# Banded attention and a gated layer on one core: a batch's sinks in one load, own slots for the last outputs, the last slice in halves

## The chip, the cores and the metric

The kernel runs on one core of a Trainium2 chip. The metric is the device time of one execution in microseconds (us). Before the change it is 776.53 us, the median of three runs (776.24 to 777.06). A difference below 0.2% (about 1.5 us) cannot be told from no change.

## The reference

Attention over 4 batches, 8 heads, 768 positions, head size 64. A query sees the first `n_sink` = 4 keys (the sinks) and a causal window of 128 keys. The head outputs, laid side by side, are the 3072 x 512 input x of a gated layer with 1536 hidden columns:

```
scores = where(is_sink | in_window, q @ k.T / 8, -1e9)
x      = (softmax(scores) @ v), heads side by side          # 3072 x 512
out    = (sigmoid(x @ w_gate) * (x @ w_val)) @ w_out        # 3072 x 512
```

The weights arrive as float64 and are decoded on the chip.

## The kernel before

Work is cut into attention units (`attend`: batch, head, 256 queries; 96 of them) and into the gated layer (`feed`) over eight chunks of tokens: four of 256, then four of 512. A feed runs over 12 slices of 128 hidden columns (`f` from 0 to `NF - 1`). Precise products are made of two parts: a tile is split into a rounded part (`hi`, `gh`) and its remainder (`lo`, `gl`), and TensorE multiplies three of the four combinations. The remainders of the weights are spilled to DRAM (`wlo_d`) and read back slice by slice into eight `lo` slots.

In the last four chunks (`feed_pair`) one slice goes as follows: 72 matmuls into the accumulators `m`; VectorE adds them up into `cv` and `th` (two halves of 256 tokens), ScalarE takes tanh of `th`; VectorE multiplies `th` and `cv`; `gated` rounds the product (`gh`) and subtracts (`gl`); `downs` multiplies `gh` and `gl` with the output weights into four accumulators (two called `o`, two called `a`, one per 128 tokens). TensorE normally works on the next slice's `m` while a slice passes through the vector engines. After the last slice, `out_tiles` copies each accumulator by ScalarE into a tile `w` (tag `w2`, two slots) and SP stores it. A small check (`bad`, `count`, `flag`, `total`) follows, with a branch that all engines take.

For each batch `sinks` loads the 16 first rows of v for all heads, repeated eight times over the 128 partitions, into `raw` (also a `w2` slot; the trace calls it `w`), from which ScalarE or VectorE and GpSimd make `vshl`.

The order of all instructions is made before the launch: `Plan.run` (lines 353 to 546) simulates the engines with a table of costs and due times and records, for each engine, the operation of lowest priority number that is ready. An operation with several `ways` goes to whichever engine is free. `GAP` sits in a rule there: an operation is held back when one that is more urgent by more than `GAP` will be due within 0.6 of its duration. An attention unit's priority is its number, so `GAP` = 2.0 compares units at least three apart. Up to 130 us the plan also puts matmuls of `ident` on TensorE where it expects the engine to be idle (`m<-ident`, fillers without use). All operations are recorded by a helper at line 618, so every row of the trace has that line.

Of the kernel before, what the change touches and what calls it, by code (L numbers as in the profile page):

```python
# [9 lines left out]
F32 = mybir.dt.float32  # L10
F32R = mybir.dt.float32r
# [4 lines left out]
ALU = mybir.AluOpType  # L16
# [4 lines left out]
NS = 16  # L21
# [3 lines left out]
CHUNKS = ((0,), (1,), (2,), (3,), (4, 5), (6, 7), (8, 9), (10, 11))  # L25
# [10 lines left out]
FLIP = 1  # L36
HOLD = 0.6
HELD = 800000.0
GAP = 2.0
LATER = 45000.0  # L40
HALVED = 30000.0
TSTEP = 8000.0
# [50 lines left out]
BUFS = {}  # L93
# [456 lines left out]
def kernel(  # L550
# [2 lines left out]
    qk: bass.AP,  # L553
    v: bass.AP,
    vt: bass.AP,
    marks: bass.AP,
    w_gate: bass.AP,
    w_val: bass.AP,
# [8 lines left out]
    B, H, S, D = v.shape  # L567
    DM, DF, _ = w_gate.shape
    DO = w_out.shape[1]
    NC = DM // 128  # L570
    NF = DF // 128
# [15 lines left out]
    class Late:  # L587
# [5 lines left out]
        def tile(self, *args, **kw):  # L593
            if self.pool is None:
                first.close()
                self.pool = main.enter_context(tc.tile_pool(name="p3", bufs=1))
            return self.pool.tile(*args, **kw)
# [10 lines left out]
    plan = Plan()  # L608

    class InOrder:  # L610
# [9 lines left out]
    PE, V, A, G, Q = (  # L620
        InOrder(e) for e in (nc.tensor, nc.vector, nc.scalar, nc.gpsimd, nc.sync)
    )
# [10 lines left out]
    def act(cols, psum=False):  # L633
        return 120 + 0.9 * cols
# [7 lines left out]
    def dma(prio, ns, fn, r=(), w=(), start=0.0, behind=None):  # L642
        return plan.op(prio, [("Q", ISSUE, fn)], r, w, dma=ns, start=start, behind=behind)
# [43 lines left out]
    def tile(shape, dtype, tag, bufs, pool=None):  # L687
# [7 lines left out]
    VSHL = {}  # L695
# [15 lines left out]
            out=nums()[:, 0:4],  # L711
            in_=marks.bitcast(I32).rearrange("(o x) -> o x", o=1).broadcast_to([128, 4]),
# [125 lines left out]
    def sinks(b, u):  # L838
        if not b:
            for y in range(2):  # L840
                for x in V0:
                    zero(u + 0.5 + y, x[y], 3 * D, lambda x=x, y=y: x[y]()[:, :, (1 - y) * D : (2 - y) * D], 4)
            for x in SK0:
                zero(u + 0.4, x, 128, x)
            for x in VS0:
                zero(u + 0.3, x, H * D, x)
            for t, x in enumerate(VS0):
                for y in range(2):
                    o = 64 * y + NS * t
                    dma(  # L850
                        u + 0.5, 91.0, lambda x=x, y=y, o=o: Q.dma_start(
                            out=x()[o : o + NS, :, y * D : y * D + D],
                            in_=v[b, y::2, 0:NS, :].rearrange("h p d -> p h d"),
                        ), w=[(x, o)],
                    )
        raw = tile([128, H, D], F32, "w2", BUFS["w2"])
        for i in range(0 if b else 1, 2):
            VSHL[b, i] = tile([128, H // 2, 2 * D], F32R, "vshl", 2, const)
        u = max(u, PLAIN) + SINKP
        for o in range(0, 128, NS):  # L860
            dma(
                u, 91.0, lambda o=o: Q.dma_start(
                    out=raw()[o : o + NS], in_=v[b, :, 0:NS, :].rearrange("h p d -> p h d"),
                ), [READY2], [(raw, o)] + [VSHL[b, i] for i in range(2) if b and (b, i) in VSHL],
            )
        for i in range(0 if b else 1, 2):
            hs = slice(i * H // 2, i * H // 2 + H // 2)
            both = VSHL[b, i]
            x, hi = lambda hs=hs: raw()[:, hs], lambda both=both: both()[:, :, 0:D]
            copy(u, H // 2 * D, hi, x, [raw], [both, READY2])  # L870
            rest(
                u, H // 2 * D, lambda both=both: both()[:, :, D : 2 * D], x, hi, [raw, both], [both]
            )
# [482 lines left out]
    def out_tiles(ci, g, T, O):  # L1356

        for j, acc in enumerate(O):
            ot = tile([128, DO], F32, "w2", BUFS["w2"])
            r = (g + j) * 128  # L1360
            plan.op(
                -1000.0 + ci + 1,
                [("A", act(DO, True), lambda acc=acc, ot=ot: A.mul(out=ot(), in_=acc(), mul=0.5))],
                [acc], [ot],
            )
            dma(ci, 728.0, lambda ot=ot, r=r: Q.dma_start(out=out[r : r + 128], in_=ot()), [ot])

    def feed(ci):
# [103 lines left out]
    def downs(pe, f, O, gh, gl, woh, wol, when):  # L1472
        for j, acc in enumerate(O):

            def down(j=j):
                ts = slice(j * 128, j * 128 + 128)
                for i, (x, w) in enumerate(((gh, woh()[:, 0]), (gh, wol()), (gl, woh()[:, 0]))):
                    PE.matmul(
                        O[j](), lhsT=x()[:, ts], rhs=w,
                        start=f == 0 and i == 0, stop=f == NF - 1 and i == 2,  # L1480
                    )

            plan.op(
                pe + when[j] / NF, [("PE", 3 * mac(DO), down)], [gh, gl, woh, wol], [acc]
            )
# [50 lines left out]
    def feed_pair(ci, tcs, f, O):  # L1536
        pr = -1000.0 + ci + f / NF
        pe = 10000.0 + ci + f / NF
        n, k = tcs
        gh_, vh_, woh, th_ = wres[f]  # L1540
        t12h, t12l, glo, tlo, vlo, wol = fetch(pr, f, 0, 1, 3, 2, 4, 5)
        ma, mb = (Tile(MS, None, F32, "m", BUFS["m"]) for _ in range(2))
        th = tile([128, 2, 256], F32, "th", BUFS["th"])
        cv = tile([128, 2, 256], F32, "cv", BUFS["cv"])
        X = lambda *key: lambda i: (XH[key]()[:, i], XL[key]()[:, i])
        xs = lambda *key: [XH[key], XL[key]]
        gw, vw, tw = (lambda i, x=x: x()[:, i] for x in (gh_, vh_, th_))
        reg = lambda m, i: lambda: m()[:, i * 256 : i * 256 + 256]
        u2, c1, t0, t1 = (lambda i=i, x=x: x()[:, i] for x in (cv, th) for i in range(2))

        def add(out, m, i, x, r, w):
            plan.op(
                pr, [("V", vec(256), lambda: V.tensor_tensor(
                    out=out(), in0=reg(m, i)(), in1=x(), op=ALU.add
                ))],
                [m] + r, w,
            )

        def turn(i, src, r):
            plan.op(  # L1560
                pr, [("A", act(256, True), lambda: A.activation(
                    out=th()[:, i], in_=src(), func=AF.Tanh, scale=0.5
                ))],
                r, [(th, i)],
            )

        product(pe, ma, 0, 256, gw, 0, four(glo), 0, X(n, 0), True, False, [gh_, glo] + xs(n, 0), [ma, GROUPS])
        product(
            pe + 0.05 / NF, ma, 1, 256, four(t12h), 2, four(t12l), 2, X(k, "s2"), False, True,
            [t12h, t12l] + xs(k, "s2"), [ma],  # L1570
        )
        plan.op(
            pr, [("A", act(256, True), lambda: A.copy(out=u2(), in_=reg(ma, 0)()))],
            [ma], [cv, th],
        )
        add(u2, ma, 1, u2, [], [(cv, 0)])
        product(
            pe + 0.2 / NF, mb, 0, 256, tw, 0, four(tlo), 0, X(k, "s3"), True, False, [th_, tlo] + xs(k, "s3"),
            [mb, GROUPS],
        )  # L1580
        product(
            pe + 0.25 / NF, mb, 1, 256, four(t12h), 0, four(t12l), 0, X(k, "s1"), False, False,
            [t12h, t12l] + xs(k, "s1"), [mb],
        )
        add(t1, mb, 0, u2, [(cv, 0)], [(th, 1)])
        add(c1, mb, 1, t1, [(th, 1)], [(cv, 1)])
        product(
            pe + 0.4 / NF, ma, 0, 256, gw, 2, four(glo), 2, X(n, 1), False, True, [gh_, glo] + xs(n, 1), [ma],
        )
        product(  # L1590
            pe + 0.45 / NF, ma, 1, 256, tw, 2, four(tlo), 2, X(k, 1), True, True,
            [th_, tlo] + xs(k, 1), [ma],
        )
        turn(0, reg(ma, 0), [ma])
        add(t1, ma, 1, t1, [], [(th, 1)])
        turn(1, t1, [])
        product(
            pe + 0.6 / NF, mb, 1, 256, vw, 2, four(vlo), 2, X(k, "s4"), False, True,
            [vh_, vlo] + xs(k, "s4"), [mb],
        )  # L1600
        add(u2, mb, 1, u2, [], [(cv, 0)])
        plan.op(
            pr, [("V", two(512), lambda: V.scalar_tensor_tensor(
                out=th(), in0=th(), scalar=1.0, in1=cv(), op0=ALU.add, op1=ALU.mult
            ))],
            [cv], [th],
        )
        gh, gl = gated(pr, 512, th)
        downs(pe, f, O, gh, gl, woh, wol, (1.3, 1.5, 1.65, 1.7))

    decoding = iter(range(3 * NF))

# [6 lines left out]
    u = 0  # L1619
# [42 lines left out]
        general(tc, qk, v, ident, nsk, win, wres, wlo_d, out)  # L1662


_INS = ["qk", "v", "vt", "marks", "moe_w_gate", "moe_w_val", "moe_w_out"]
_OUTS = [((3072, 512), "float32")]


# [40 lines left out]
```

## Time and profile before

| what | value |
|---|---|
| median of three runs | 776.53 us |
| the profiled execution | 771.55 us |
| its span, first to last instruction | 769.8 us |
| TensorE busy, VectorE, ScalarE, GpSimd | 97%, 79%, 62%, 66% |
| granted TensorE clock, mean of the span | 0.997 |
| end of SP's last store issue (758.96 + 3.78), end of the span | 762.74, 769.8 us |

The profiled execution took 771.55 us, of which 1.75 us lie outside the span. It is 4.98 us below the median of the timed runs. The busy share of TensorE is read by stages: an engine that is busy nearly all the time can only be helped where it waits.

### The profile page before, as it was taken

Reading aid. Unit: us, or ns where it says so; the run is one execution under the profiler, and the core shown is the slowest. Engines: PE = TensorE matmul, PEld = TensorE weight load, DVE = VectorE, ACT = ScalarE, POOL = GpSimd, SP = SyncE. Lnnn points to the kernel's source line nnn. Section 1 sums busy time; section 2 is a strip of 40 time slices with the busy share of each in tenths; the row PEclk is TensorE's granted clock in tenths of the full one; section 3 lists DMA queues with packets and bytes.
Section 4 is the critical chain, followed back from the end, with each engine's and each line's share of the span. In section 5 each row is a group of like instructions: output and inputs, shape, how many; then the busy total and the mean of one; then the engine's idle time right before and its main releaser. Section 6 shows DMA issues by size and latency. Waiting matters only on the chain.

```text
span 769.8 us, 16294 instructions
## 1 busy us (share of the span) xinstructions
PE 747.2 (97%) x4986; PEld 675.6 (88%) x4986; DVE 606.8 (79%) x1776; ACT 473.4 (62%) x1339; POOL 507.1 (66%) x648
## 2 busy tenths in 40 slices
PE   7999999999999999999999999999999999999994
PEld 6867777999899999989999989999999999999993
DVE  5979988987899999969988999689999874433331
ACT  7889898756765777647666665467776642322221
POOL 3664677887999989847787977467976854412120
PEclk9999999999999999999999999999999999999998
DMA  6898987999999876677767776867687656776661
GB/s 165 230 293 262 335 270 237 374 310 303 337 327 311 271 236 203 207 249 234 242 217 222 248 250 198 255 210 237 208 290 243 179 170 209 226 227 205 199 198 59
DMA packets 120878, 185.57 MB, mean 241 GB/s; under 512 B 23248, under 2 KB 45264, under 8 KB 120784
## 3 DMA queue, kind: packets, MB, share of 16 engines
q1 hardware_dynamic: 120784, 184.45, 75.9%
q8 instruction: 42, 0.69, 0.4%
q14 instruction: 52, 0.43, 0.2%
HBM read 159.24 MB, written 25.17 MB: 240 GB/s over the span
## 4 chain that ended last, share of the span: by engine, by line
PE 67%; DVE 10%; DMA 4%; ACT 2%; POOL 2%; issue 1%; SPq 0%; ACTq 0%; POOLq 0%; DVEq 0%
PE m L618 37%; PE a L618 18%; PE o L618 12%; DMA out_dram<-w 1%; DVE ws L618 1%; DVE P L618 1%; DVE th L618 1%; POOL wt L618 1%; DMA wst<-in_moe_w_gate_dram 1%; DVE hi L618 1%; DVE gl L618 1%; DVE vhl L618 1%; DMA wst<-in_moe_w_out_dram 1%; DMA lo<-wlo_d 1%; DVE xf L618 1%
## 5 line engine op out<-in xcount | busy, mean ns | idle before, releaser
L618 PE MATMUL m<-ws,lo 128*128 128x256 f32 x1344 | 288.4, 283 | 1.7 <-DMA lo<-wlo_d 0.9
L618 PE MATMUL m<-ws,ws 128*128 128x256 f32 x1536 | 289.3, 284 | 0.2 <-ACT th L618 0.2
L618 PEld LDWEIGHTS m<-ws,ws 128*128 128x128 f32 x1536 | 245.1, 189 | 12.1 <-issue 0.5
L618 PEld LDWEIGHTS m<-ws,lo 128*128 128x128 f32 x1344 | 215.0, 189 | 2.7 <-DMA lo<-wlo_d 1.7
L618 POOL TENSOR_SCALAR_AFFINE_SELECT wt<-wt 128x512 fp32r<-128x512 f32 (+3 forms) x192 | 124.7, 651 | 42.9 <-DVE wt L618 18.7
L618 POOL TENSOR_TENSOR gl<-th,gh 128x512 fp32r<-128x512 f32 (+1 forms) x35 | 39.3, 1124 | 105.7 <-ACT gh L618 88.7
L618 ACT ACTIVATE P<-P,negm_all 128x144 f32<-128x144 f32 x192 | 78.9, 411 | 29.4 <-DVE negm_all L618 27.7
L618 ACT ACTIVATE th<-m 128x256 f32<-128x256 f32 x96 | 36.6, 381 | 74.7 <-DVE th L618 71.1
L618 DVE TENSOR_TENSOR cv<-m,cv 128x256 f32<-128x256 f32 x96 | 40.1, 418 | 51.0 <-ACT cv L618 33.0
L618 ACT CAST gh<-th 128x512 fp32r<-128x512 f32 (+1 forms) x81 | 42.7, 527 | 52.9 <-DVE th L618 51.1
L618 POOL TENSOR_TENSOR ws<-ws,ws 128x512 fp32r<-128x512 f32 (+1 forms) x53 | 66.9, 1270 | 8.3 <-DVE ws L618 5.5
L618 PE MATMUL o<-ws,gh 128*128 128x512 f32 x168 | 67.7, 403 | 1.3 <-ACT w L618 0.7
L618 PE MATMUL o<-ws,gl 128*128 128x512 f32 x168 | 66.2, 394 | 0.7 <-POOL gl L618 0.7
L618 PE MATMUL o<-lo,gh 128*128 128x512 f32 x168 | 65.8, 392 | 0.0
L618 DVE CUSTOM_DVE_ANT_0 P<-a,am 128x144 f32<-128x144 f32 x192 | 58.3, 306 | 9.2 <-PE a L618 2.6
L618 PE MATMUL a<-wt,vhl 128*128 128x256 f32 (+2 forms) x282 | 60.9, 326 | 0.2
L618 POOL TENSOR_TENSOR kl<-qkT,hi 128x400 fp32r<-128x400 f32 (+1 forms) x56 | 58.8, 1050 | 1.8
L618 ACT CAST hi<-qkT 128x656 fp32r<-128x656 f32 (+1 forms) x70 | 49.2, 703 | 10.5 <-PE a L618 8.6
L618 PEld LDWEIGHTS a<-wt,vhl 128*128 128x128 f32 x282 | 47.3, 189 | 8.5 <-POOL wt L618 2.2
L618 POOL TENSOR_TENSOR P<-P,rs 128x288 f32<-128x288 f32 x46 | 35.5, 774 | 28.5 <-DVE rs L618 24.6
L618 POOL TENSOR_TENSOR hi<-qkT,hi 64x256 fp32r<-64x256 f32 x53 | 41.6, 784 | 14.0 <-issue 3.2
L618 DVE COPY_PREDICATED a<-tri,a 128x128 f32<-128x128 int32 x160 | 45.4, 284 | 3.8 <-PE a L618 3.4
(142 smaller groups left out, 1737.8 us busy)
## 6 DMA issues: line engine op xcount, KB each, us to landing
lo<-wlo_d SPq DMA_DIRECT2D x396, 256.0 KB, 3.7
wlo_d<-ws SPq DMA_DIRECT2D x72, 256.0 KB, 4.3
qkT<-in_qk_dram SPq DMA_DIRECT2D x52, 328.0 KB, 4.2
qkT<-in_qk_dram SPq DMA_DIRECT2D x24, 264.0 KB, 3.8
wst<-in_moe_w_gate_dram SPq DMA_DIRECT2D x12, 512.0 KB, 4.6
wst<-in_moe_w_val_dram SPq DMA_DIRECT2D x12, 512.0 KB, 5.2
wst<-in_moe_w_out_dram SPq DMA_DIRECT2D x12, 512.0 KB, 5.2
out_dram<-w SPq DMA_DIRECT2D x24, 256.0 KB, 3.9
```

The source lines that it names most:

```text
L618: return lambda *a, **kw: tc.keep_in_program_order(op(*a, **kw))
```

## The change

Four edits.

1. The host passes one more array, `vs`: for each batch the 16 sink rows of all heads, 2 KB per row, repeated eight times to 128 rows. `sinks` loads it by one DMA of 128 rows instead of eight DMAs of 16 x 8 pieces of 256 bytes.
2. The outputs of the last chunk go to `xf` slots (five) instead of `w2` (two), and may be copied by VectorE as well as by ScalarE.
3. The last slice of the last chunk goes through multiply, round and subtract in two halves of 256 tokens (second half first), the subtraction on VectorE; the twelve output matmuls are ordered by half, the `gh` ones ahead of the `gl` ones.
4. `GAP` is 1.5 instead of 2.0, so that the rule also compares units two apart.

```
-GAP = 2.0
+GAP = 1.5
...
-        for o in range(0, 128, NS):
-            dma(
-                u, 91.0, lambda o=o: Q.dma_start(
-                    out=raw()[o : o + NS], in_=v[b, :, 0:NS, :].rearrange("h p d -> p h d"),
-                ), [READY2], [(raw, o)] + [VSHL[b, i] for i in range(2) if b and (b, i) in VSHL],
-            )
+        dma(
+            u, 728.0, lambda: Q.dma_start(out=raw(), in_=vs[b].rearrange("p (h d) -> p h d", h=H)),
+            [READY2], [raw] + [VSHL[b, i] for i in range(2) if b and (b, i) in VSHL],
+        )
...
-            ot = tile([128, DO], F32, "w2", BUFS["w2"])
+            last = ci == len(CHUNKS) - 1
+            ot = tile([128, DO], F32, *(("xf", BUFS["xf"]) if last else ("w2", BUFS["w2"])))
...
+            ways = [
+                ("A", act(DO, True), lambda acc=acc, ot=ot: A.mul(out=ot(), in_=acc(), mul=0.5)),
+                (
+                    "V", vec(DO), lambda acc=acc, ot=ot: V.tensor_scalar(
+                        out=ot(), in0=acc(), scalar1=0.5, scalar2=None, op0=ALU.mult
+                    ),
+                ),
+            ]
+            plan.op(-1000.0 + ci + 1, ways if last else ways[:1], [acc], [ot])
...
+        if ci == len(CHUNKS) - 1 and f == NF - 1:
+            last_slice(pr, pe, O, th, cv, woh, wol)
+            return
...
+    def last_slice(pr, pe, O, th, cv, woh, wol):
+
+        gh = tile([128, 512], F32R, "gh", BUFS["gh"])
+        gl = tile([128, 512], F32R, "gl", BUFS["gl"])
+        for h in (1, 0):
+            cs = slice(h * 256, h * 256 + 256)
+            t = lambda h=h: th()[:, h]
+            plan.op(
+                pr, [("V", two(256), lambda h=h, t=t: V.scalar_tensor_tensor(
+                    out=t(), in0=t(), scalar=1.0, in1=cv()[:, h], op0=ALU.add, op1=ALU.mult
+                ))],
+                [(cv, h)], [(th, h)],
+            )
+            hi, lo = lambda cs=cs: gh()[:, cs], lambda cs=cs: gl()[:, cs]
+            plan.op(
+                pr, [("A", act(256), lambda hi=hi, t=t: A.copy(out=hi(), in_=t()))],
+                [(th, h)], [(gh, h)],
+            )
+            plan.op(
+                pr, [("V", two(256), lambda hi=hi, lo=lo, t=t: V.tensor_tensor(
+                    out=lo(), in0=t(), in1=hi().bitcast(F32), op=ALU.subtract
+                ))],
+                [(th, h), (gh, h)], [(gl, h)],
+            )
+        n = 0
+        for h in (1, 0):
+            for x, ws in ((gh, (lambda: woh()[:, 0], lambda: wol())), (gl, (lambda: woh()[:, 0],))):
+                for j in (2 * h, 2 * h + 1):
+
+                    def down(j=j, x=x, ws=ws):
+                        for w in ws:
+                            PE.matmul(
+                                O[j](), lhsT=x()[:, j * 128 : j * 128 + 128], rhs=w(),
+                                start=False, stop=x is gl,
+                            )
+
+                    n += 1
+                    plan.op(
+                        pe + (1.7 + 0.01 * n) / NF, [("PE", len(ws) * mac(DO), down)],
+                        [(x, h), woh, wol], [O[j]],
+                    )
```

Edits 1 and 4 alter the plan's inputs near the start, and nearly the whole order of the instructions on every engine comes out differently. Work moves between engines that share an operation (of the full-width subtractions `gl`, 25 stand on VectorE before and 19 after), the stores and loads keep their number but for the sinks (32 loads become 4), and the fillers go from 26 to 31 (each is two rows of the trace).

TensorE at the end of the program, before; `o` and `a` are the four accumulators, `gh` and `gl` the rounded part and the remainder of the last slice, `ws` and `lo` the output weights:

```order
L618 MATMUL a_10523<-ws_1765,gl_11270 128x512
L618 MATMUL o_10474<-ws_2039,gh_11325 128x512
L618 MATMUL o_10474<-lo_11249,gh_11325 128x512
L618 MATMUL o_10474<-ws_2039,gl_11327 128x512
L618 MATMUL o_10500<-ws_2039,gh_11325 128x512
L618 MATMUL o_10500<-lo_11249,gh_11325 128x512
L618 MATMUL o_10500<-ws_2039,gl_11327 128x512
L618 MATMUL a_10515<-ws_2039,gh_11325 128x512
```

The same place after; `a_10486` and `a_10494` hold the second half of the tokens:

```order
L619 MATMUL a_10486<-ws_1967,gh_11293 128x512
L619 MATMUL a_10486<-lo_11220,gh_11293 128x512
L619 MATMUL a_10494<-ws_1967,gh_11293 128x512
L619 MATMUL a_10494<-lo_11220,gh_11293 128x512
L619 MATMUL o_10445<-ws_1967,gh_11293 128x512
L619 MATMUL o_10445<-lo_11220,gh_11293 128x512
L619 MATMUL a_10486<-ws_1967,gl_11302 128x512
L619 MATMUL a_10494<-ws_1967,gl_11302 128x512
L619 MATMUL o_10471<-ws_1967,gh_11293 128x512
L619 MATMUL o_10471<-lo_11220,gh_11293 128x512
L619 MATMUL o_10445<-ws_1967,gl_11302 128x512
L619 MATMUL o_10471<-ws_1967,gl_11302 128x512
```

A matmul of `gl` stood third before; now six matmuls of `gh` come ahead of the first one.

VectorE at the end, before; the multiply of the last slice is the third row:

```order
L618 TENSOR_TENSOR th_11290<-m_89,th_11290 128x256
L618 TENSOR_TENSOR cv_11278<-m_90,cv_11278 128x256
L618 SCALAR_TENSOR_TENSOR th_11290<-th_11290,cv_11278 128x512
L1656 CAST flag<-count 1x4
L1658 TENSOR_REDUCE total<-flag 1x1
```

The same place after:

```order
L619 TENSOR_TENSOR th_11261<-m_89,th_11261 128x256
L619 SCALAR_TENSOR_TENSOR th_11261<-th_11261,cv_11249 128x256
L619 TENSOR_TENSOR cv_11249<-m_90,cv_11249 128x256
L619 SCALAR_TENSOR_TENSOR th_11261<-th_11261,cv_11249 128x256
L619 TENSOR_TENSOR gl_11302<-th_11261,gh_11293 128x256 x2
L619 TENSOR_SCALAR xf_11311<-a_10486 128x512
L619 TENSOR_SCALAR xf_11320<-o_10445 128x512
L1705 CAST flag<-count 1x4
L1707 TENSOR_REDUCE total<-flag 1x1
```

The first half's multiply stands ahead of the last sum `cv`, both subtractions and two of the four output copies are VectorE's now, and the check's `flag` waits behind them. ScalarE keeps the two roundings and the other two copies.

SP's queue around the first batch's sinks, before (`w_210` is `raw`, `qkT` and `vhl` are loads of the attention):

```order
L618 DMA wst_204<-in_moe_w_out_dram 128x1024
L618 DMA w_210<-in_v_dram 16x8x64 x3
L618 DMA qkT_160<-in_qk_dram 64x528
L618 DMA w_210<-in_v_dram 16x8x64
L618 DMA vhl_111<-in_vt_dram 128x2x64
L618 DMA qkT_98<-in_qk_dram 64x528
L618 DMA w_210<-in_v_dram 16x8x64
L618 DMA vhl_153<-in_vt_dram 128x2x64
L618 DMA w_210<-in_v_dram 16x8x64 x3
L618 DMA qkT_116<-in_qk_dram 64x528
```

The same place after:

```order
L619 DMA wst_204<-in_moe_w_out_dram 128x1024
L619 DMA w_210<-in_vs_dram 128x512
L619 DMA qkT_164<-in_qk_dram 64x528
L619 DMA vhl_111<-in_vt_dram 128x2x64
L619 DMA qkT_98<-in_qk_dram 64x528
L619 DMA vhl_153<-in_vt_dram 128x2x64
L619 DMA qkT_116<-in_qk_dram 64x528
```

One load of 256 KB stands where three of 32 KB stood, and the five that stood between the attention's loads are gone.

## Rows read from the trace of the kernel before

**Rows 1.** The page, engines: busy us (share of the span) and instructions.
```profile
PE 747.2 (97%) x4986; PEld 675.6 (88%) x4986; DVE 606.8 (79%) x1776; ACT 473.4 (62%) x1339; POOL 507.1 (66%) x648
```
**Rows 2.** Windows: length, busy us (instructions) per engine, PEclk, DMA share, GB/s.
```profile
0.00:50.00 50.00, 43.69 (x244) 36.97 (x245) 36.15 (x150) 40.49 (x110) 26.47 (x51) 1.00 0.82 221
50.00:130.00 80.00, 77.89 (x359) 58.18 (x358) 72.39 (x191) 72.39 (x140) 48.73 (x55) 1.00 0.86 273
130.00:500.00 370.00, 366.36 (x2590) 340.24 (x2589) 329.65 (x965) 240.09 (x746) 299.84 (x385) 1.00 0.82 264
500.00:750.00 250.00, 249.96 (x1750) 233.11 (x1749) 165.61 (x466) 116.76 (x339) 130.83 (x158) 1.00 0.69 216
750.00:769.80 19.80, 9.32 (x52) 7.12 (x50) 3.00 (x8) 3.70 (x7) 1.28 (x1) 0.88 0.16 57
```
**Rows 3.** Waits of TensorE, whole span: us in total, times, longest.
```profile
PE a L618 <- POOL P L618: 2.0, 3, 1.2
PE a L618 <- DMA qkT<-in_qk_dram: 1.6, 1, 1.6
...
PE a L618 <- DVE P L618: 0.2, 1, 0.2
```
**Rows 4.** Timeline of the end: start us, us, engine, operation, [idle before <-releaser].
```profile
753.85 0.41 ACT L618 ACTIVATE th<-th 128x256 f32<-128x256 f32 x1
...
754.46 0.42 DVE L618 TENSOR_TENSOR cv<-m,cv 128x256 f32<-128x256 f32 x1 [0.98 <-PE m L618]
...
754.99 0.69 DVE L618 SCALAR_TENSOR_TENSOR th<-th,cv 128x512 f32<-128x512 f32 x1
...
755.42 0.40 PE L618 MATMUL a<-ws,gl 128*128 128x512 f32 x1
755.71 0.62 ACT L618 CAST gh<-th 128x512 fp32r<-128x512 f32 x1 [1.45 <-DVE th L618]
...
756.38 0.50 PE L618 MATMUL o<-ws,gh 128*128 128x512 f32 x1 [0.57 <-ACT gh L618]
756.46 1.28 POOL L618 TENSOR_TENSOR gl<-th,gh 128x512 fp32r<-128x512 f32 x1 [6.49 <-ACT gh L618]
...
757.79 0.50 PE L618 MATMUL o<-ws,gl 128*128 128x512 f32 x1 [0.67 <-POOL gl L618]
...
758.96 3.78 SPq L618 DMA_DIRECT2D out_dram<-w  x4
...
759.97 0.40 PE L618 MATMUL a<-ws,gl 128*128 128x512 f32 x1
761.09 1.29 ACT L618 ACTIVATE w<-a 128x512 f32<-128x512 f32 x2 [1.47 <-DMA out_dram<-w]
...
762.16 0.15 DVE L1658 TENSOR_REDUCE total<-flag 1x1 int32<-1x4 int32 x1
```
**Rows 5.** Groups by shape: count, busy us, mean ns of one, idle before.
```profile
L618 DVE TENSOR_TENSOR cv<-m,cv 128x256 f32<-128x256 f32 x96 | 40.1, 418 | 51.0 <-ACT cv L618 33.0 <-PE m L618 17.3
...
L618 DVE TENSOR_TENSOR gl<-th,gh 128x256 fp32r<-128x256 f32 x24 | 17.6, 732 | 2.0 <-PE o L618 1.0 <-ACT gh L618 0.9
...
L618 ACT CAST gh<-th 128x256 fp32r<-128x256 f32 x35 | 14.1, 404 | 15.5 <-DVE th L618 14.8
...
L618 PE MATMUL m<-ident 128*128 128x128 f32 x52 | 9.9, 317 | 1.4 <-POOL ident masks.py:199 1.4
```
**Rows 6.** Waits of SP's own queue, 758 us to the end.
```profile
SPq L1661 <- SPq L1661: 4.1, 1, 4.1
```
**Rows 7.** The tile w, SP's issues: ns min/median/max, first and last start.
```profile
L618 SPq DMA_DIRECT2D w<-in_v_dram x32: 311/424/1371, 10.4 to 493.6; - x32
L618 SPq DMA_DIRECT2D out_dram<-w x24: 332/338/602, 130.7 to 762.4; - x24
```
**Rows 8.** Windows, as rows 2, while the first sinks arrive.
```profile
17.50:18.00 0.50, 0.00 (x0) 0.00 (x0) 0.00 (x0) 0.03 (x1) 0.28 (x1) 1.00 0.32 68
```
**Rows 9.** The same view, a stretch of bulk loads.
```profile
130.00:140.00 10.00, 10.00 (x75) 9.13 (x74) 8.64 (x22) 7.98 (x23) 8.70 (x10) 1.00 1.00 370
```

More of the change, by code (lines that the diff above doesn't have):

```diff
@@ L555 @@
     vt: bass.AP,
+    vs: bass.AP,
     marks: bass.AP,
@@ L1358, in out_tiles @@
         for j, acc in enumerate(O):
-            ot = tile([128, DO], F32, "w2", BUFS["w2"])
+            last = ci == len(CHUNKS) - 1
+            ot = tile([128, DO], F32, *(("xf", BUFS["xf"]) if last else ("w2", BUFS["w2"])))
             r = (g + j) * 128
[L1361 to L1365, printed above, removed]
+            ways = [
[7 more added lines that the diff above has]
+            plan.op(-1000.0 + ci + 1, ways if last else ways[:1], [acc], [ot])
             dma(ci, 728.0, lambda ot=ot, r=r: Q.dma_start(out=out[r : r + 128], in_=ot()), [ot])
@@ L1662 @@
         general(tc, qk, v, ident, nsk, win, wres, wlo_d, out)
-_INS = ["qk", "v", "vt", "marks", "moe_w_gate", "moe_w_val", "moe_w_out"]
+_INS = ["qk", "v", "vt", "vs", "marks", "moe_w_gate", "moe_w_val", "moe_w_out"]
 _OUTS = [((3072, 512), "float32")]
@@ L1688 @@
     vt = v.reshape(*v.shape[:2], v.shape[2] // 128, 128, v.shape[3]).transpose(0, 1, 3, 2, 4)
-    made = {"qk": qk, "vt": vt, "marks": _np.array([inputs["n_sink"], inputs["window"]], _np.int64)}
+    vs = _np.tile(v[:, :, 0:NS].transpose(0, 2, 1, 3).reshape(v.shape[0], NS, -1), (1, 128 // NS, 1))
+    made = {"qk": qk, "vt": vt, "vs": vs, "marks": _np.array([inputs["n_sink"], inputs["window"]], _np.int64)}
     for name in _INS:
```

## The prediction

> **What bounds the kernel now.** I read the busy shares first, then the same by stages, then TensorE's waits, then the end of the timeline. TensorE is busy 97% of the span [rows 1], so only its idle time can be won. By stages [rows 2] it idles 6.3 us in the first 50 us (50 - 43.69), 2.1 us from 50 to 130, 3.6 us from 130 to 500, and nothing from 500 to 750 (0.04 us). After 750 it works 9.32 of 19.8 us. [...] The waits of TensorE [rows 3] are small and of many kinds: the list has 16 entries, of which I show the first two and the last, 21 waits together of 14.1 us. Three (2.7 us) belong to the end and one (1.4 us) to the start; 17 waits of 10.0 us, 0.59 us each, lie in the body. The reader is to see that no single releaser bounds the body, while the end is one chain.
>
> The end [rows 4]: TensorE ends the eleventh slice's last matmul, started 755.42, and could go on 0.24 us later, the distance at which such matmuls follow each other (759.97 is the ninth start after 757.79). It waits for the rounding `gh`, itself behind a sum (754.46) and a full-width multiply (754.99), and starts at 756.38; then for `gl` on GpSimd (756.46 + 1.28), and starts at 757.79. Its last matmul starts at 759.97. Two output copies go at once, the third starts at 761.09 because its slot is freed by the first store's landing. SP ends its fourth issue at 758.96 + 3.78 = 762.74, so it starts it 0.34 us [rows 7] earlier, at 762.40. The check's `total` ends at 762.31. From there it is 7.4 to 7.5 us to the span's end, where SP waits 4.1 us at the branch on nothing but itself [rows 6]; the engines' DMA and compute rows are empty there.
>
> **The change part by part.**
>
> *Last slice.* The tanh of the second half ends at 754.26 [rows 4]. VectorE's half multiply: 0.69 us is the full one [rows 4], a 256-column sum takes 0.42 [rows 5]; I take 0.40, between 0.35 (half of 0.69) and 0.42. It runs 754.30 to 754.70, in front of the last sum, which so moves from 754.46 to 754.73 and ends 755.15; the other multiply ends 755.58. ScalarE's half roundings take 0.40 [rows 5]: 754.75 to 755.15, and 755.62 to 756.02. The first subtraction also waits until TensorE has read the single `gl` slot of the slice before (755.82), and takes between 0.35 (half the full multiply) and 0.73 us; 0.73 is the mean of a mix beside a busy GpSimd [rows 5], which here stands idle, so I take 0.42, like the sum: `gl` of the second half is there at 756.28, of the first at 756.74.
>
> TensorE: twelve matmuls at 0.24 us from 755.66, start numbers 0 to 11. Number 0 needs the first rounding (755.15, there), number 4 (756.62) the second (756.02), number 6 (757.10) the first remainder, number 10 (758.06) the second. All are early, by 0.5 us or more; at 0.73 us per subtraction they come at 756.59 and 757.32, still early. The last start is 755.66 + 11 x 0.24 = 758.30, against 759.97: -1.7 us. The stall goes into nothing new, since two roundings and two subtractions lie beside matmuls.
>
> [...]
>
> *Outputs.* Accumulator two is complete after number 6 (757.10 + 0.40 = 757.50), the next after number 7 (757.74), then after 10 (758.46) and 11 (758.70). A copy by ScalarE takes 0.60 us (two in 1.29, rows 4). Half of a 512-column copy from an accumulator by VectorE is between 0.21 and 0.42 us if a 256-column sum [rows 5] bounds it, so the whole is 0.42 to 0.84; I take 0.65, near ScalarE's. VectorE: 757.54 to 758.19, and 758.50 to 759.15. ScalarE: 757.78 to 758.38, and 758.74 to 759.34. No copy waits for a slot: five `xf` slots, long free. The fourth store is issued at 759.37 instead of 762.40 (-3.0), the first three lie before it at 0.34 us each. `total` stands behind VectorE's second copy: 759.15 + about 0.4 for flag and total (0.15 each, rows 4) = 759.5 instead of 762.31 (-2.8). With 0.84 us copies it is 759.7 (-2.6).
>
> Which of the two sets the end is nearly a tie before, so the one that gains less counts: -2.8 us, range -2.4 to -3.2. The 4.1 us behind the branch I carry over, as rows 6 name no other releaser.
>
> *Sinks.* Per batch SP issues one load instead of eight of 0.42 us: 7 x 0.42 = 3.0 us of SP time free, four times. On the DMA engines pieces of 256 bytes arrive at 68 GB/s with a share of 0.32 [rows 8], so 213 GB/s if they filled it; bulk loads reach 370 GB/s at a share of 1.00 [rows 9]. 256 KB cost 1.2 us before, 0.7 after. Whom does it help? The first batch's sinks stand before the load of `qkT` on which TensorE waits 1.6 us [rows 3]. Before, three pieces of 32 KB (0.46 us) are ahead of it, after, the whole 256 KB (0.71 us): 0.25 us later. The five pieces further back (0.77 us) vanish before later loads. The bounds are -1.6 us (the wait goes) and +0.25; I take 0, since the loads ahead in the queue, those of the weights, stay. The later sinks are read by ScalarE well before TensorE needs them; TensorE has no wait on them, so I cost them at 0. If that cover is gone, the price is a wait like those of rows 3, which the last term holds.
>
> *Fillers.* 31 instead of 26: five more, ten rows of at most 9.9/52 = 0.19 us [rows 5], 0 to 1.9 us. They stand where the plan expects TensorE idle, and rows 3 show that it does idle for GpSimd's `P` there. I take +0.2.
>
> *The new order, `GAP` included.* All engines' orders change, and from 500 us on nothing can be won. The 17 waits of the body are drawn anew. Their number and size stay what TensorE's fixed work and the same loads make them, so the mean is 0. If each is independent, with 0.59 us mean and about 0.4 us spread (0.2 to 1.6, rows 3), their sum scatters by sqrt(17 x (0.59^2 + 0.4^2)) = 2.9 us. The bounds are -10.0 us (all go) and about +10 (twice as many); I use the scatter.
>
> *Sum.* -2.8 + 0 + 0.2 + 0 = -2.6 us. Against its own time the profiled execution goes from 771.55 to 768.95 us (span 767.2). The timed runs lie 4.98 us above the profiled one, and I move their median by the same amount: 776.53 - 2.6 = 773.9 us.
>
> **The rivals.**
>
> *The body gets better too.* The new order closes two or three waits, say the `qkT` wait of 1.6 us and another of 1.2: -2.6 - 2.8, 771.1 us. For it: SP and the DMA engines are relieved in the stage with the most idle time [rows 2]. Against: the long waits there are for GpSimd and ScalarE as well.
>
> *The gain is eaten.* The new order opens waits of 1.2 to 4.2 us in all, and the time is 776.5 us. For it: seventeen waits have to fall just as well by chance. Against: nothing in the diff adds a wait on purpose.
>
> *Slower: the first 130 us starve.* There VectorE and ScalarE are busy 72 of 80 us from 50 us on [rows 2], so an order that serves an attention unit late cannot catch up. `GAP` 1.5 holds operations back more often, which leaves a loaded engine idle, and the plan itself sets five more fillers. Price: fillers in full 1.9 us, and two more waits as long as the longest (1.6 each) make +5.1 - 2.8 = +2.3, 778.8 us. It decides from 4.4 us more idle time in 0 to 130 us, where it is 8.4 now. Against: the same rule serves the more urgent unit sooner, on which TensorE waits.
>
> *The end does not follow.* If the 4.1 us at the branch were tied to something other than the branch's own start, the end would gain less, down to 0: 776.7 us. No row ties it, so I count it with the eaten gain.
>
> **How the numbers follow.** Forecast (the body within about 1.2 us): 0.42. Better: 0.25. Eaten: 0.21. Slower: 0.12. A measurement of this kernel tells 0.2%, 1.55 us, from no change. Faster is forecast and better, 0.67; same 0.21; slower 0.12. The likeliest case's own range is 772.7 to 775.0. The range leaves out the better half of "better" and most of "slower": 769.8 to 777.8 us.
>
> **What would show it.** In the profile after: TensorE without a gap between the slices at the end, its last matmul starting about 2.6 us after the first `gh` one; no wait of ScalarE on a store; the four stores issued within 1.5 us; from the last issue to the span's end still about 7.4 us; SP's waits at the branch still about 4 us. For the body: idle time of TensorE of 6, 2, 4 and 0 us in the same stages. I am wrong if the first 130 us idle 4 us more or less, if matmuls of `gl` wait for VectorE, or if the last 7.4 us grow.

## The result and the profile after

The changed kernel takes 780.55 us, the median of 20 runs (778.09 to 784.85), against 776.65 us for the kernel before in as many runs of the same comparison (773.37 to 780.39). The ratio is 1.0056, with a 95% interval of 1.0041 to 1.0071: slower by 0.56%, about 4.3 us. The ratio is not the quotient of the two medians, which lie 3.9 us apart; where a ratio is given in us below, it is the ratio's distance from 1 times the time before. One execution of the kernel before, among those that the first four experiments are held against, took 2480.33 us and is left out of their ratios. I had predicted 773.9 us and a range that ended at 777.8.

The profiled execution took 781.51 us (span 779.8), near its median. That of before, 771.55 us, is shorter than each of its own 20 timed runs. So the two traces lie 10.0 us apart in their spans, the medians only 3.9 us, and what the pair of traces shows must be held against other executions of the same orders.

The end first. The timeline of the changed kernel from the eleventh slice's last matmul on [rows 4]; the columns are those of rows 4:

```profile
768.30 0.39 PE L619 MATMUL a<-ws,gl 128*128 128x512 f32 x1
768.43 0.41 ACT L619 CAST gh<-th 128x256 fp32r<-128x256 f32 x1 [0.38 <-DVE th L619]
768.53 0.39 PE L619 MATMUL a<-ws,gh 128*128 128x512 f32 x1
...
768.83 0.76 DVE L619 TENSOR_TENSOR gl<-th,gh 128x256 fp32r<-128x256 f32 x2 [0.43 <-ACT gh L619]
...
770.33 0.69 DVE L619 TENSOR_SCALAR xf<-a 128x512 f32<-128x512 f32 x1 [0.75 <-PE a L619]
770.37 0.39 PE L619 MATMUL o<-ws,gh 128*128 128x512 f32 x1
770.56 0.60 ACT L619 ACTIVATE xf<-a 128x512 f32<-128x512 f32 x1 [1.73 <-PE a L619]
770.60 0.39 PE L619 MATMUL o<-lo,gh 128*128 128x512 f32 x1
770.83 0.63 PE L619 MATMUL o<-ws,gl 128*128 128x512 f32 x2
771.05 1.80 SPq L619 DMA_DIRECT2D out_dram<-xf  x4
...
772.04 0.14 DVE L1707 TENSOR_REDUCE total<-flag 1x1 int32<-1x4 int32 x1
```

The new slice starts 0.23 us behind the old one and has no gap; no copy waits for a store. The last matmul starts at 770.83 + 0.63 - 0.40 = 771.06, 2.76 us after the slice before it (4.55 in [rows 4]); the fourth store is issued at 771.05 + 1.80 - 0.40 = 772.45, 4.15 us after (6.98); `total` ends 3.88 us after (6.89). From 768.30 to the span's end there are 11.5 us, against 14.4 before (769.8 - 755.42). SP's wait at the branch stayed nearly as long, 3.7 us against 4.1 [rows 6]; here it is among its waits at the end:

```profile
SPq L1710 <- SPq L1710: 3.7, 1, 3.7
```

So the end gained 2.9 us, and everything before it lost 12.9 us in this pair of traces. The engines' line of the page [rows 1] and the windows by stage [rows 2], after:

```profile
PE 751.5 (96%) x4996; PEld 675.9 (87%) x4996; DVE 614.0 (79%) x1781; ACT 470.4 (60%) x1333; POOL 509.5 (65%) x646
```

```profile
0.00:50.00 50.00, 45.28 (x258) 38.71 (x258) 35.80 (x147) 39.89 (x109) 26.96 (x51) 1.00 0.73 207
50.00:130.00 80.00, 75.00 (x335) 54.14 (x336) 67.88 (x173) 68.60 (x135) 46.83 (x55) 1.00 0.87 269
130.00:500.00 370.00, 361.40 (x2535) 332.53 (x2534) 343.95 (x1019) 252.11 (x784) 309.89 (x399) 1.00 0.79 261
500.00:750.00 250.00, 248.27 (x1735) 231.28 (x1734) 156.79 (x425) 103.74 (x294) 123.28 (x140) 1.00 0.67 214
```

TensorE's idle time by stage is 4.7, 5.0, 8.6 and 1.7 us; before it was 6.3, 2.1, 3.6 and 0.0, and I had forecast 6, 2, 4 and 0. The clock is at 1.00 throughout. Of the 12.9 us, 8.0 show as idle time up to 750 us. The other 4.9 stand as more busy time ahead of the last slice (748.24 us up to 768.30, against 743.32 up to 755.42 before), of which the ten more filler matmuls are 0.9 us by the groups [rows 5]:

```profile
L619 PE MATMUL m<-ident 128*128 128x128 f32 x62 | 10.8, 313 | 1.4 <-POOL ident masks.py:199 1.4
```

Most of the rest belongs to the waits as well, for a wait costs more than its idle time. In [rows 4] TensorE idles 0.57 us before 756.38, but the matmul starts 0.72 us later than the step of 0.24 us would have it, and the next one follows after 0.35 us. I estimate the whole cost by holding each step from one matmul's start to the next against the median step of its shape over the traces of this case. From the first matmul up to 750 us, TensorE was interrupted 28 times before and 46 times after, the short ones included that the list of waits leaves out, for 15.9 and 27.7 us, of which only 10.7 and 18.6 are idle time. The difference, 11.8 us, and the ten fillers at 0.11 us per step make up the 12.9.

The waits of TensorE over the whole span [rows 3], after:

```profile
PE m L619 <- DVE th L619: 3.1, 6, 0.8
PE o L619 <- DVE th L619: 2.8, 4, 1.0
...
PE m L619 <- DVE cv L619: 1.4, 2, 1.0
PE a L619 <- DMA qkT<-in_qk_dram: 0.9, 1, 0.9
PE o L619 <- DVE gl L619: 0.9, 2, 0.7
```

Before, the list was led by GpSimd and a load. Now 14 waits of 8.2 us are for tiles of the gated layer that VectorE makes: `th`, `cv` and `gl`. Before, one wait of the body was:

```profile
PE o L618 <- DVE th L618: 0.7, 1, 0.7
```

Counted as the prediction counts them, without the start and the end, the body's 17 waits of 10.0 us became 29 of 17.3 us: their mean stayed, 0.59 and 0.60 us, and their number rose.

### The profile page after: what moved, and what is told of

Same layout as the page of the kernel before. It is cut to its first block, busy times and chain, and to the rows that moved or that the text cites. A ratio compares the mean times of both kernels' runs of the same rounds, so it can differ in the third digit from the quotient of the medians.

```text
span 779.8 us, 16242 instructions
## 1 busy us (share of the span) xinstructions
PE 751.5 (96%) x4996; PEld 675.9 (87%) x4996; DVE 614.0 (79%) x1781; ACT 470.4 (60%) x1333; POOL 509.5 (65%) x646
## 4 chain that ended last, share of the span: by engine, by line
PE 65%; DVE 8%; DMA 6%; POOL 4%; issue 1%; ACT 1%; SPq 0%; POOLq 0%; DVEq 0%; ACTq 0%
PE m L619 36%; PE a L619 17%; PE o L619 11%; DMA lo<-wlo_d 3%; DVE ws L619 2%; DMA out_dram<-w 1%; DMA wst<-in_moe_w_out_dram 1%; DVE vhl L619 1%; POOL wt L619 1%; DVE th L619 1%; DVE gl L619 1%; DVE xf L619 1%; POOL kl L619 1%; DMA vraw<-in_vt_dram 1%; DVE hi L619 1%
## 5 line engine op out<-in xcount | busy, mean ns | idle before, releaser
L619 POOL TENSOR_SCALAR_AFFINE_SELECT wt<-wt 128x512 fp32r<-128x512 f32 (+3 forms) x192 | 127.0, 663 | 38.8 <-DVE wt L619 17.8
L619 POOL TENSOR_TENSOR gl<-th,gh 128x512 fp32r<-128x512 f32 (+1 forms) x35 | 42.2, 1207 | 111.2 <-ACT gh L619 104.3
L619 POOL TENSOR_TENSOR ws<-ws,ws 128x512 fp32r<-128x512 f32 (+1 forms) x52 | 64.8, 1254 | 15.5 <-DVE ws L619 11.2
L619 POOL TENSOR_TENSOR P<-P,rs 128x288 f32<-128x288 f32 x52 | 40.0, 769 | 30.3 <-DVE rs L619 27.2
L619 POOL TENSOR_TENSOR hi<-qkT,hi 64x256 fp32r<-64x256 f32 x57 | 45.4, 797 | 12.1 <-DVE hi L619 4.9
L619 ACT CAST hi<-qkT 128x656 fp32r<-128x656 f32 (+1 forms) x66 | 46.2, 701 | 2.8 <-PE a L619 2.1
```

The costliest lines, as they stand in the source:

```text
L619: return lambda *a, **kw: tc.keep_in_program_order(op(*a, **kw))
```

## The experiments

Four theories. ORDER: the body's change is a fresh draw of the instruction order, and the order of before is a favourable one. GAP: the stricter rule costs by itself. LOAD: one load of 256 KB delays what is behind it. And, for single waits, QUEUE: such a wait comes from what stands in front of a late operation in an engine's queue, and against it STORE: the operation would have come late anyway. Ratios are to the kernel before on the same chip, with 95% intervals.

**The edits one by one.** The tail alone (edits 2 and 3 in full, all else in the order of before):

```
-            ot = tile([128, DO], F32, "w2", BUFS["w2"])
+            ot = tile([128, DO], F32, *(("xf", BUFS["xf"]) if last else ("w2", BUFS["w2"])))
...
+        if ci == len(CHUNKS) - 1 and f == NF - 1:
+            last_slice(pr, pe, O, th, cv, woh, wol)
+            return
```

> Before with edits 2 and 3 alone (own slots for the last outputs, last slice in halves); the order of every engine is that of before up to the last slice. All theories: the end gains what the trace of after shows, 2.9 us (from the eleventh slice's last matmul to the span's end 11.5 us instead of 14.4), so 773.8 us or -0.37%. If the gain were an artefact of another body: 776.6 us.

Measured: 0.9973 (0.9950 to 0.9997), 772.80 us against 775.69: -2.1 us by the ratio, -2.9 by the medians. The tail's edits do what was predicted, together: halves, the subtraction on VectorE instead of GpSimd and the order by half were not tried one by one.

`GAP` alone:

```
-GAP = 2.0
+GAP = 1.5
```

> Before with edit 4 alone (GAP 1.5). Theory GAP (holding operations back leaves VectorE and ScalarE idle while TensorE waits): +5 to +9 us, 782 to 786 us. Theory ORDER (any other order draws TensorE's waits anew, and this draw was bad): not tied to GAP, anywhere from -3 to +8 us. Theory LOAD (one load of 256 KB in place of eight of 32 KB delays what stands behind it): 0, 776.6 us.

Measured: 1.0057 (1.0033 to 1.0080). This one number alone costs as much as the whole change. That fits GAP and ORDER alike.

Edits 1 to 3 with `GAP` = 2.0:

> After with GAP back at 2.0 (edits 1 to 3). Theory GAP: 773.8 us, the gain at the end alone. Theory LOAD: as after, about 780.5 us. Theory ORDER: the order is a third one; the body anywhere from -3 to +8 us, so 771 to 782 us.

Measured: 1.0002 (0.9981 to 1.0023). The 773.8 us of GAP and the 780.5 us of LOAD are missed. With the tail's -2.1 us in it, the rest is some +2 us, which the two intervals don't tell from zero, though the rule is the old one: edit 1 alone also gives a new order.

The sinks by one load, with the seven other places kept empty in the plan, so that every engine keeps the order of before:

```
-                u, 91.0, lambda o=o: Q.dma_start(
-                    out=raw()[o : o + NS], in_=v[b, :, 0:NS, :].rearrange("h p d -> p h d"),
+                u, 91.0, lambda o=o: None if o else Q.dma_start(
+                    out=raw(), in_=vs[b].rearrange("p (h d) -> p h d", h=H),
```

> Before, its order kept on every engine, with the sinks by one load at the place of the first of the eight (the other seven places are empty). Theory LOAD: +3 us or more, with a longer wait of TensorE on qkT at about 17 us. Theories GAP and ORDER: within 1 us of before, 775.6 to 777.6 us.

Measured: 0.9989 (0.9967 to 1.0010). LOAD falls: the load itself costs nothing that can be measured. Its trace shows the wait for `qkT` 0.6 us longer than before, in the waits of TensorE up to 50 us:

```profile
PE a L619 <- DMA qkT<-in_qk_dram: 2.2, 1, 2.2
```

In a later run with the same load and the same order (below) it is 1.6 us again, so this difference is not the load's.

**Is it the rule, or any new order?** Four kernels in which one planning number differs and nothing else. `LAT` is the plan's delay, 180 ns, from the end of an operation to its use on another engine.

```
-LAT = 180.0
+LAT = 181.0
```

> Before with one planning number moved by a hair (LAT 181 instead of 180 ns), GAP 2.0: another order on every engine, with no rule changed. Theory ORDER (before's order is a good draw, and any other order loses on average): +2 to +6 us over before. Theory GAP (the stricter rule costs): within 1.5 us of before.

Measured: 1.0065 (1.0039 to 1.0091).

The same with `LAT = 179.0`:

> As the run before it with LAT 179: one more draw. Theory ORDER: +2 to +6 us over before. Theory GAP: within 1.5 us of before.

Measured: 1.0020 (1.0000 to 1.0039), +1.6 us: between the two theories.

The kernel before with `GAP = 1.99`, which among attention units, whose priorities are whole numbers, compares the same ones as 1.5 (other operations have fractions, and from 27 us on the order is not that of 1.5 either):

> Before with GAP 1.99 (1.9 gives the same order): of what 1.5 adds to the rule, this takes attention units exactly two apart, and leaves out the fractional distances between 1.5 and 1.9. Theory GAP: +4 us, as with 1.5 alone (+4.4). Theory ORDER: a draw, from 0 to +6 us.

Measured: 1.0014 (0.9994 to 1.0034).

And with `GAP = 2.5`, the looser direction:

> Before with GAP 2.5, a looser rule: fewer operations are held back. Theory GAP: not slower than before (-2 to +0.5 us). Theory ORDER: a draw, +2 to +6 us.

Measured: 1.0047 (1.0029 to 1.0065). A number moved by 0.5% with no rule touched costs as much as the stricter rule, and the looser rule costs too. GAP as the cause falls here; whether it has a smaller price of its own needs pairs.

**Pairs, and the order held.** All of the change's other edits in the order of before (the lines of the first and the fourth experiment together):

> Edits 1, 2 and 3 of the change (one load of the sinks, own output slots, last slice in halves) with GAP 2.0 and the sinks' other seven places kept empty in the plan, so that all engines run the order of before up to the last slice. ORDER (the body's change of time is a fresh draw of the order, and the order of before is a favourable draw): the tail's gain stays whole, -2.1 to -2.9 us against before, about -0.3%, and 6 to 8 us below the changed kernel's own distance to before (+4.3). GAP (the stricter rule is what costs): the same. LOAD (one big load delays what is behind it): +1 us or more above the run with the tail's edits alone (0.9973), so 0 or slower against before.

Measured: 0.9944 (0.9921 to 0.9968), 771.15 us against 776.06. This version beats both kernels, by more than the 2.1 to 2.9 us expected; its interval, -6.1 to -2.5 us, holds them. Against the changed kernel, which does the same work but for the ten more filler matmuls in another order, it stands at 0.9944 / 1.0056 = 0.9889: the order makes 1.1%, some 8.7 us.

`GAP = 1.5` with `LAT = 181.0`, the pair of 1.0065:

> The kernel before with LAT 181 instead of 180 and GAP 1.5: the pair of the run with LAT 181 and GAP 2.0, which took +0.65% (+4.7 us). GAP (the stricter rule costs 4 us of its own, as it does at LAT 180): about +8.5 us against before, 1.0110. ORDER (any change of the plan's numbers draws a new order, the rule's direction has no price): unrelated to its pair, between 0 and +6 us, as likely below the pair's +4.7 as above.

Measured: 1.0017 (0.9995 to 1.0039).

`GAP = 1.5` with `LAT = 179.0`, the pair of 1.0020:

> The same pair at LAT 179, where GAP 2.0 took +0.2% (+1.7 us). GAP: about +6 us, 1.0075. ORDER: between 0 and +6 us, unrelated to its pair.

Measured: 1.0044 (1.0018 to 1.0070). The stricter rule adds 0.57% at `LAT` 180, takes off 0.48% at 181 and adds 0.24% at 179, each to about 0.3%: the first two are clear of zero, and the sign hangs on a number that has nothing to do with the rule.

`LAT = 180.2`, all else as before:

> The kernel before with LAT 180.2 instead of 180: one planning number moved by 0.1%, no rule touched; the order comes out different from the first rows on. GAP (a rule that does not change costs nothing): within 0.2% of before. ORDER, with before's order a favourable draw: slower by 0 to 5 us, about +3, like the other draws.

Measured: 1.0125 (1.0088 to 1.0162), 785.14 us. ORDER holds in sign, but the size is beyond the 5 us that I had given it: the slowest draw of all comes from a number moved by 0.1%. Its trace sets my expectation right in one thing: by operation, tile and shape, every engine's rows are those of before up to 136 us, and TensorE idles 8.3 us up to 130 us against 8.4. All that this draw loses it loses behind that. Its granted clock, 0.993 to 0.997 in its six runs, is within that of before, 0.991 to 0.998, so the clock is not the reason.

The eight draws that leave the work as it was, but for up to ten filler matmuls (0.9 us) more (1.0057, 1.0065, 1.0020, 1.0014, 1.0047, 1.0017, 1.0044, 1.0125) have a mean of 1.0049 and a standard deviation of 0.0036, in time +3.8 us and 2.8 us. The mean is known to about 0.0030, so it isn't zero, and all eight lie above 1.

Where the orders differ is plainest in the last long stage. The window from 500 to 750 us of the kernel with the held order, and then of the slowest draw:

```profile
500.00:750.00 250.00, 249.98 (x1749) 233.20 (x1748) 165.75 (x467) 116.86 (x338) 129.66 (x157) 1.00 0.69 217
```

```profile
500.00:750.00 250.00, 246.90 (x1720) 229.44 (x1720) 167.66 (x468) 118.11 (x343) 128.71 (x152) 1.00 0.68 212
```

The order of before has no idle time there in any of its four profiled executions (of the kernel before and of the first, fourth and ninth experiment; 0.02 to 0.04 us each); ten fresh orders have 0.0 to 3.1 us, 1.1 in the mean. Up to 750 us the idle time is 15.1 us in the mean of the four (12.1 to 19.5) and 18.1 us in that of the ten (15.9 to 21.5): these ranges overlap, and only the last stage tells the orders apart.

**What one such wait is made of.** In the changed kernel TensorE waits 0.97 us at 582 us. Its timeline there:

```profile
580.85 0.60 ACT L619 ACTIVATE w<-a 128x512 f32<-128x512 f32 x1 [2.21 <-DMA out_dram<-w]
581.34 0.37 ACT L619 COPY cv<-m 128x256 f32<-128x256 f32 x1
581.74 0.42 DVE L619 TENSOR_TENSOR cv<-m,cv 128x256 f32<-128x256 f32 x1 [1.29 <-ACT cv L619]
582.22 0.51 PE L619 MATMUL m<-ws,ws 128*128 128x256 f32 x2 [0.97 <-DVE cv L619]
```

The last output copy of the sixth chunk waits 2.21 us for a `w2` slot that a store still holds. The copy `cv<-m` stands behind it in ScalarE's order and starts when it is through; VectorE's sum waits for that copy (1.29 us) and TensorE for the sum (0.97 us). In the order of before the same two stand the other way round; ScalarE of the kernel with the held order:

```profile
564.79 0.38 ACT L619 COPY cv<-m 128x256 f32<-128x256 f32 x1
565.20 0.60 ACT L619 ACTIVATE w<-a 128x512 f32<-128x512 f32 x1
```

To test it, the sixth chunk's outputs got `xf` slots too, in the changed kernel; up to there the order stays:

```
-("xf", BUFS["xf"]) if last else
+("xf", BUFS["xf"]) if last or ci == 5 else
```

> The changed kernel with own output slots (xf) for the sixth chunk too, whose outputs are copied near 577 to 581 us; up to there the order is the one of the changed kernel, behind it a new one. QUEUE (a single wait of a redrawn order comes from what stands in front of a late operation in an engine's queue: here ScalarE's output copy, which waits for a store's landing for 2.2 us with the copy cv<-m behind it): ScalarE's wait there goes, TensorE's 0.97 us wait for cv at 582 us goes with it, and the median falls by about 1 us against the changed kernel, 1.0043 against before, plus or minus what the order behind it draws. STORE (the copy waits, but cv would have come late anyway because VectorE or TensorE were behind): ScalarE's wait goes and TensorE's wait at 582 us stays within 0.3 us.

Measured: 1.0047 (1.0027 to 1.0066). The sixth chunk's copies wait for no store any more, and among TensorE's waits from 500 to 750 us the one for `cv` is gone:

```profile
576.14 1.23 ACT L619 ACTIVATE xf<-a 128x512 f32<-128x512 f32 x2 [0.42 <-PE a L619]
...
578.22 0.35 ACT L619 COPY cv<-m 128x256 f32<-128x256 f32 x1
```

```profile
PE m L619 <- DMA lo<-wlo_d: 0.6, 1, 0.6
PE a L619 <- POOL P L619: 0.4, 1, 0.4
PE a L619 <- DVE xf L619: 0.2, 1, 0.2
```

The same edit in the slowest draw, where TensorE waits 1.04 us at 576 us behind a copy that waits 1.5 us:

> The same edit to the slowest draw, the kernel before with LAT 180.2 (1.0125), where TensorE waits 1.04 us for cv at 576 us behind a ScalarE copy that waits 1.5 us for a store. QUEUE: this wait goes, and the median falls by about 1 us, to 1.011, plus or minus what the order behind it draws. STORE: TensorE's wait for cv stays.

Measured: 1.0102 (1.0080 to 1.0124). Here too the wait for `cv` is gone; TensorE's idle time of that stage falls from 3.1 us to 1.2. QUEUE holds, STORE falls: both waits were made by a copy that stood ahead of `cv<-m` on ScalarE and waited for its slot. The place behind the copies stayed in both runs; with nothing to wait for there, it cost nothing. Against the kernels without the edit, 1.0056 and 1.0125, the 0.1% and 0.2% gained are too little to be told from zero.

The waits for `th` have another front. VectorE, ScalarE and TensorE of the changed kernel near 151 us:

```profile
149.66 0.42 DVE L619 TENSOR_TENSOR wt<-a,wt 128x256 fp32r<-128x256 f32 x1
...
149.99 0.68 DVE L619 TENSOR_TENSOR ws<-ws,ws 128x512 fp32r<-128x512 f32 x1
...
150.59 0.16 DVE L619 RECIPROCAL rs<-rs 128x2 f32<-128x2 f32 x1
150.67 0.40 DVE L619 SCALAR_TENSOR_TENSOR th<-th,m 128x256 f32<-128x256 f32 x1
...
151.12 0.50 PE L619 MATMUL m<-ws,ws 128*128 128x256 f32 x2 [0.83 <-DVE th L619]
```

VectorE goes without a pause through an attention tile, a remainder of the weights and a reciprocal before it reads the accumulator `m` that TensorE wants back. This one wasn't taken away by a run, so its cause is read, not shown.

## Why the prediction was wrong

*The end: right.* Predicted -2.8 us (range -2.4 to -3.2); the trace shows -2.9, the tail alone -2.1 by the ratio (interval -3.9 to -0.2) and -2.9 between the medians. The terms: VectorE's half multiplies 0.42 us (0.40 taken), half subtractions 0.42 with GpSimd idle (0.42; the 24 of before [rows 5] had GpSimd busy beside them, all or part of the time, and took 0.38 to 1.50; the 0.76 of the two are shorter than their sum because they overlap), half roundings 0.41 (0.40), VectorE's output copy 0.69 (0.65, between bounds of 0.42 and 0.84). The last matmul gained 1.8 us (1.7), the fourth store 2.8 (3.0), `total` 3.0 (2.8). The stall went into nothing new, the twelve matmuls follow each other without a gap, and the stretch from the last issue to the end stayed (7.35 us, 7.4 before), so "the end does not follow" falls. The halves lie beside matmuls, so their extra cost stayed hidden: the two half multiplies take 0.85 us together (0.43 and 0.42) against 0.69 for the whole, the two half roundings 0.81 (0.405 and 0.408) against 0.62 [rows 4].

*Sinks: right.* Costed at 0; with the order held they measure 0.9989 (0.9967 to 1.0010), which leaves room for -2.6 to +0.8 us.

*Fillers: small.* +0.9 us of busy time in the trace, 1.1 us from start to start (0.2 taken, bound 1.9).

*The new order: the step that failed.* I wrote that the waits' "number and size stay what TensorE's fixed work and the same loads make them, so the mean is 0". The size stayed, the number didn't: 17 waits of 0.59 us became 29 of 0.60. And the mean of the draws is +3.8 us, not 0. That their scatter, 2.8 us, comes out at the 2.9 us forecast is partly luck, since it was worked out from 17 independent waits, from idle time alone, and the 2.8 us contain the error of the runs.

Two reasons for the mean stand in the rows that I had. First, I took the waits of one order as a sample of what any order has. But they are that order's own, and the stage from 500 to 750 us, a third of the span, had none [rows 2]: I noted that nothing could be won there and didn't go on that a new order can only lose there. In idle time this is 1.1 us of the mean; where the rest of the +3.8 arises is not settled by these traces. Second, I took their number to follow from work and loads, though a wait can hang on what stands ahead of a late operation in its engine's order. That is shown for two waits, one of them 0.97 us of the changed kernel's 8.2 us for `th`, `cv` and `gl`; for the other thirteen it is not.

The changed kernel is then the end's -2.1 to -2.9 us and a draw of +6 to +7 us (8.7 against the held order). Of that draw 3.8 us are the mean that I had put at 0; the other 2 to 3 are bad luck of the size of the scatter.

*The profile I started from.* It showed 2.1 us of idle time from 50 to 130 us, and I forecast the same. Its own order has 5.4, 4.4 and 3.2 us there in three other executions (the latter two with the sinks by one load): the value was that execution's. Over the body it had 17 waits of 10.0 us, the other three 21 to 23 of 12.3 to 17.5 us, so it was also a good execution of a good order. One trace is too little to forecast idle time by stages.

*The rivals.* "Slower: the first 130 us starve" had the sign and nearly the size (778.8 us), but not the place. TensorE idles 9.7 us there after the change, 1.3 us more and not the 4.4 from which that rival decides; the order of before idles 8.4, 11.8, 10.4 and 9.5 us. And the slowest draw keeps the order of before up to 136 us. The window of 0 to 130 us of the kernel with the tail alone, which is the second of these and one of the fastest kernels:

```profile
0.00:130.00 130.00, 118.21 (x590) 92.82 (x591) 107.20 (x332) 110.70 (x245) 72.29 (x103) 1.00 0.84 249
```

*What stays open.* Why the order of before is better than its neighbours isn't seen in any run, nor how its planning numbers were chosen, nor whether far better ones exist. A small price of `GAP` = 1.5 isn't excluded: four pairs (three of `LAT`, and edits 1 to 3 with and without it) give +0.57, -0.48, +0.24 and +0.54%, mean +0.2%, which such scatter doesn't tell from zero. And of the changed kernel's 29 waits in the body two were followed to their start, and one of these was taken away by a run.

## What to carry to other kernels

Where a planner or a scheduler sets the order, any edit upstream of it is two edits: what it does, and a new draw of the order. Price the draw against the order that you have: stages without idle time can only lose, so the mean of the draw need not be zero. Price a wait by more than its idle time: here 28 interruptions cost an estimated 15.9 us, of which 10.7 were idle. Measure the edit with the order held still, and if it gains there, keep the order or try several; here the same load and the same tail come, but for ten filler matmuls, with -0.56% in one order and +0.56% in the other.

## What the runs showed of the hardware

One order of instructions doesn't have one set of waits. The kernel before took 773.15 to 782.35 us in 29 runs on one chip, a spread of 1.2%, and the granted clock doesn't tell the two apart, 0.998 in the fastest and 0.997 in the slowest. TensorE idled, in one and the same order, between 8.4 and 11.8 us in the first 130 us of four executions. With a dozen runs the ratios' intervals reach about 0.25% to either side; a difference of a few microseconds between two profiles settles nothing until a second execution shows it.
